# Feed-forward weight tiles laid out in DRAM along the loop, and three loads moved on the issue queue of a recurrent transformer block

## The chip, the cores and the metric

The kernel runs on one core of one Trainium2 chip. The metric is the device time of one launch in microseconds (us), as a median over several runs. The engines are TensorE (PE in the profile; PEld is its weight load), VectorE (DVE), ScalarE (ACT), GpSimd (POOL) and SyncE (SP), which here only issues DMAs.

## The reference

The input is one sequence of 2048 rows of 640 numbers in bf16. A pre-norm block is computed: recurrent attention over 64 segments of 32 rows, then a gated feed-forward part, each with a residual.

```python
x = A_x
h = x + _A_ref(_layernorm(x), A_mem0, A_Wq, A_Wk, A_Wv, A_Wo, 32)
h2 = h + _B_ref(_layernorm(h), B_W_gate, B_W_up, B_W_down)

def _A_ref(x, mem0, Wq, Wk, Wv, Wo, seg_len):      # 32 heads of 128
    mem = mem0                                      # 8 rows
    for s in range(n_seg):                          # 64 segments, one after the other
        h = concatenate([mem, xs], axis=1)          # 8 + 32 rows
        q, k, v = h @ Wq, h @ Wk, h @ Wv            # per head
        p = softmax(where(mask, q k^T * scale, -1e9))
        o = (p v) @ Wo
        mem = o[:, :M, :]                           # the next segment's memory
        outs.append(o[:, M:, :])

def _B_ref(x, W_gate, W_up, W_down):                # 640 -> 1728 -> 640
    gate = x @ W_gate
    return ((gate * (gate > 0)) * (x @ W_up)) @ W_down
```

Segment s needs the 8 memory rows that segment s-1 has put out, so the 64 segments are a chain.

## The kernel before, in words

A setup part loads the attention weights (W for Q, K and V, and Wo) into SBUF, where they stay, and computes segment 0. Then comes a loop over the steps s = 1 to 63, one segment each. After it the feed-forward part runs over four blocks of 512 rows.

**A step.** Each step projects K, Q and V for the segment (`project`, line 417; 390 is the same with another weight load), multiplies Q with K (`scores`, line 513), takes exponentials, and multiplies the probabilities of the memory rows with V (`pv_mem`, line 567). Then Wo is applied to the memory rows (`wo_split`, line 632, and `wo_pass`, line 615), and the result becomes the memory rows of the next step. The segment's own rows are not urgent: their probabilities meet V in `pv_x` (line 710), early in the next step, which reads V out of a rearranged copy called VM. Three DMAs (`merge_v(s, 0)`) write VM out of Vp as soon as V of the step is there, and where s % 4 = 2 three more (`merge_v(s, 1)`) write the other part out of Ve.

**Groups of four.** The last 8 rows of segments are projected four segments at a time, in steps where TensorE would otherwise wait, and wait in Ke, Qe and Ve. There are two sets of these: set 0 has tiles of its own, set 1 lies in one tile called ends. `place(s)` tells which set a step uses. Where s % 4 = 1, the step also turns a block of 128 normalized rows over (`flip_rows(at, xl)`, a DMA transpose), then loads the next rows into xl, and multiplies the last four segments' ends with Wo (`woe_pass`); the sum goes from the tile Pbd to DRAM by two DMAs (`woe_store`, called here the Pbd stores). `store_attn` stores the attention rows of every step by four DMAs.

**Feed-forward work inside the loop.** Nine pairs of tiles of the gate and up weights (128 of 1728 columns each) are multiplied with the first 512 normalized rows already in the loop, in steps 50, 51, 52, 54, 55, 56, 58, 59 and 60 (EARLY_STEPS; `early_product`, line 916). For that the 512 rows (xn2_d in DRAM, 5 chunks) are loaded over a set of Ke, Qe and Ve that is not in use: `early_rows` in the steps before, 49, 53 and 57. `early_weights(s, 0)` loads a gate tile into xt, `early_weights(s, 1)` an up tile into at (into xl in the last three). Each reads 640 rows of 256 bytes out of a weight matrix. The product with all chunks of the gate tile stands after the first `pv_mem`, the first chunk of the up tile after the second one, and the rest after `wo_pass`. As the row loads destroy what Ke, Qe and Ve held, saved copies in DRAM are brought back: K and Q by `load_next(q, n)` out of next_d, V out of farvw_d or nextv_d, in steps 53 and 57.

**What sets the order.** Every operation is given to one list in the order of the program. Each engine carries out its own part of that list in order; waits on semaphores are worked out from what the operations read and write (`_Graph.solve`). All DMAs inside the loop are issued by SyncE (line 355, transposes 378), so a DMA whose wait isn't over holds up every later one. One of them has its place tied by hand: the load behind `first_exp` (`after`) waits for the first exponential of its step.

**DRAM-to-DRAM copies.** Some copies run from DRAM to DRAM along the loop and stand at the end of their steps: four for the last 64 columns of gate and up (wt_d, steps 3, 6, 7, 10) and three that build farvw_d (steps 11, 14, 15).

## Time and profile before

| | before |
|---|---|
| median of 3 runs | 978.67 us (977.9 to 978.81) |
| profiled execution | 980.6 us, span 978.9 us |
| TensorE busy, share of the span | 954.4 us, 98% |
| VectorE / ScalarE / GpSimd busy | 74% / 53% / 19% |
| granted TensorE clock | 1.00 |
| DMA: moved, share of 16 engines | 89.00 MB, mean 91 GB/s; SyncE's queue 30.1% |

The profile gives one execution. A busy time counts an engine's instructions; a wait is an idle stretch, put down to whatever ended it. "issue" is idle time that ended without anything the profile shows. The chain that ended last is the work followed back from the last instruction, at each step to what released it. In a list in order of time the first column is the start in us from the span's start and the second the length; SPq is SyncE's issuing of a DMA, whose landing comes later. In a table of stretches the columns are the stretch, its length, each engine's busy time with its number of instructions, the granted clock, the share of the 16 DMA engines, and GB/s.

### The profile page before, as it was taken

Reading aid. Unit: us, or ns where it says so; the run is one execution under the profiler, and the core shown is the slowest. Engines: PE = TensorE matmul, PEld = TensorE weight load, DVE = VectorE, ACT = ScalarE, POOL = GpSimd, SP = SyncE. Lnnn points to the kernel's source line nnn. Section 1 sums busy time; section 2 is a strip of 40 time slices with the busy share of each in tenths; the row PEclk is TensorE's granted clock in tenths of the full one; section 3 lists DMA queues with packets and bytes.
Section 4 is the critical chain, followed back from the end, with each engine's and each line's share of the span. In section 5 each row is a group of like instructions: output and inputs, shape, how many; then the busy total and the mean of one; then the engine's idle time right before and its main releaser. Section 6 shows DMA issues by size and latency. Waiting matters only on the chain.

```text
span 978.9 us, 56709 instructions
## 1 busy us (share of the span) xinstructions
PE 954.4 (98%) x26155; PEld 532.9 (54%) x24915; DVE 726.8 (74%) x2041; ACT 522.7 (53%) x1326; POOL 186.7 (19%) x424
## 2 busy tenths in 40 slices
PE   4899999999999999999999999999999999999998
PEld 1245555556565556665556565656565655344443
DVE  3568888888888888888888888887887884445232
ACT  1466666666666666666666666655555553122120
POOL 7021112121313131313131313020201110000000
PEclk9999999999999999999999999999999999999999
DMA  9951212222232223222232323142424247704000
GB/s 362 416 219 51 46 46 44 55 43 64 50 74 52 65 55 62 57 68 57 63 60 57 61 57 61 37 101 62 133 60 132 61 131 234 263 18 98 21 14 28
DMA packets 94708, 89.00 MB, mean 91 GB/s; under 512 B 57386, under 2 KB 78066, under 8 KB 92402
## 3 DMA queue, kind: packets, MB, share of 16 engines
q1 hardware_dynamic: 92736, 84.41, 30.1%
q8 instruction: 201, 3.29, 1.5%
q10 hardware_dynamic: 1730, 0.96, 0.4%
q14 instruction: 41, 0.34, 0.1%
HBM read 47.80 MB, written 12.27 MB: 61 GB/s over the span
## 4 chain that ended last, share of the span: by engine, by line
PE 93%; SPq 4%; DMA 3%; issue 0%; DVE 0%; POOL 0%; ACT 0%; POOLq 0%
PE ps L417 46%; PE ps L1041 9%; PE ps L615 7%; PE ps L390 7%; PE ps L632 7%; PE ps L681 4%; SPq L355 4%; PE ps L1364 3%; PE ps L916 3%; PE ps L513 3%; PE ps L710 2%; DMA Wo<-in_A_Wo_dram 2%; PE ps L567 1%; PE ps L1054 0%; DMA VM<-Vp 0%
## 5 line engine op out<-in xcount | busy, mean ns | idle before, releaser
L417 PE MATMUL ps<-W,act_r 128*32 128x512 bf16 (+1 forms) x8335 | 466.1, 360 | 0.7 <-issue 0.4
L417 PEld LDWEIGHTS ps<-W,act_r 128*32 128x32 bf16 x8335 | 217.3, 96 | 168.4 <-issue 22.8
L441 ACT ACTIVATE tok<-ps 128x512 bf16<-128x512 f32 x184 | 106.4, 594 | 62.6 <-PE ps L417 48.7
L441 ACT ACTIVATE tox<-ps 128x512 bf16<-128x512 f32 x138 | 81.8, 598 | 60.9 <-PE ps L417 50.2
L436 DVE STREAM_TRANSPOSE Ko<-tox 128x512 bf16<-128x512 bf16 x128 | 89.0, 697 | 29.7 <-ACT tox L441 29.0
L417 PE MATMUL ps<-W,act_e 128*32 128x512 bf16 x1008 | 97.0, 382 | 4.3 <-DVE TBf L494 1.9
L595 DVE STREAM_TRANSPOSE oT<-tox 128x512 bf16<-128x512 bf16 x128 | 95.2, 744 | 0.0
L436 DVE STREAM_TRANSPOSE Qo<-tok 128x512 bf16<-128x512 bf16 x124 | 85.5, 690 | 2.0 <-ACT tok L441 1.2
L615 PE MATMUL ps<-Wo,oT 128*32 128x160 bf16 x4032 | 81.9, 233 | 2.1 <-DMA Wo<-in_A_Wo_dram 1.1
L632 PE MATMUL ps<-Wo,oT 128*32 128x320 bf16 x2016 | 79.9, 299 | 0.4 <-DVE oT L589 0.4
L615 PEld LDWEIGHTS ps<-Wo,oT 128*32 128x32 bf16 x4032 | 70.3, 97 | 13.0 <-DMA Wo<-in_A_Wo_dram 3.0
L441 ACT ACTIVATE Vp<-ps 128x512 bf16<-128x512 f32 x127 | 75.1, 592 | 0.5 <-ACT Vp L441 0.5
L390 PE MATMUL ps<-W,act_e 128*32 128x512 bf16 x712 | 70.1, 383 | 0.0
L1069 ACT ACTIVATE g<-ps 128x512 bf16<-128x512 f32 x43 | 25.0, 594 | 78.3 <-PE ps L1041 76.8
L648 ACT ACTIVATE SA<-TA 64x40 f32<-64x40 f32 x126 | 29.6, 235 | 65.2 <-DVE TA L645 64.5
L529 ACT ACTIVATE Pm<-ps 128x64 bf16<-128x64 f32 x126 | 28.3, 224 | 67.6 <-PE ps L513 66.4
L589 DVE STREAM_TRANSPOSE oT<-om 128x128 bf16<-128x128 bf16 x126 | 39.3, 312 | 31.1 <-ACT om L581 31.1
L513 PE MATMUL ps<-Qo,Ko 128*32 128x40 bf16 x2048 | 61.4, 181 | 0.0
L632 PEld LDWEIGHTS ps<-Wo,oT 128*32 128x32 bf16 x2016 | 50.9, 96 | 18.2 <-DVE rm L579 0.8
L513 PEld LDWEIGHTS ps<-Qo,Ko 128*32 128x32 bf16 x2048 | 46.7, 94 | 25.5 <-DVE Qo L436 18.0
L521 POOL COPY Qo<-ends 128x256 bf16<-128x256 bf16 x32 | 14.1, 439 | 239.9 <-DVE oT L589 232.8
L521 POOL COPY Qo<-Qe 128x256 bf16<-128x256 bf16 x32 | 14.2, 444 | 231.6 <-DVE oT L589 231.6
(156 smaller groups left out, 1550.1 us busy)
## 6 DMA issues: line engine op xcount, KB each, us to landing
VM<-Vp SPq DMA_DIRECT2D x126, 65.0 KB
VM<-Vp SPq DMA_DIRECT2D x63, 130.0 KB
W<-in_A_Wk_dram SPq DMA_DIRECT2D x5, 1024.0 KB
W<-in_A_Wq_dram SPq DMA_DIRECT2D x5, 1024.0 KB
W<-in_A_Wv_dram SPq DMA_DIRECT2D x5, 1024.0 KB
Wo<-in_A_Wo_dram SPq DMA_DIRECT2D x8, 640.0 KB
attn_d<-wtok SPq DMA_DIRECT2D x248, 7.5 KB
xt<-in_A_x_dram SPq DMA_DIRECT2D x16, 160.0 KB
```

Of the source, the lines that this page charges most:

```text
L355: add(eng, lambda e: e.dma_start(dst, src), r=r, w=w, dma=True)
L390: return pe.add_instruction(mybir.InstMatmult(name=nc.get_next_instruction_name(), engine=mybir.EngineType.PE, ins=[pe.lower_ap(rhs), pe.l ...
L417: ins = pe.matmul(*b, start=(c == ends[0]), stop=(c == ends[1]), skip_group_check=True)
L436: add("dve", lambda v: v.transpose(dst[:, 16 * i:16 * i + 16, 0:32], tok[t][:, :].rearrange("p (h f) -> p h f", f=32)), r=tok_keys(t), w=keys)
L441: add("act", lambda a: a.activation(dst, src, ACTF.Copy), r=r, w=w)
L513: i = pe.matmul(bank((P0, P1)[hf])[q:q + 32, o:o + 40], (Ko if a == 0 else Ke[p])[:, h, :], Qo[:, h, :], start=True, stop=True, skip_group ...
L589: add("dve", lambda v: v.transpose(ap(oT[par], 160 * hf, [[40, 4], [320, 4], [1, 8]]), ap(om, 128 * hf, [[1, 4], [4, 32]])), r=[("om", hf) ...
L595: add("dve", lambda v, kh=kh: v.transpose(ap(oT[p], 160 * kh + M, [[320, 4], [40, 4], [1, 32]]), ap(tox, 128 * kh, [[256, 4], [1, 4], [4, ...
L615: i = pe.matmul(bank(bk)[32 * gg:32 * gg + 32, 0:160], src[:, hb, 0:32], w[:, gg], start=(hb == CH[16 * halves[0]]), stop=(hb == CH[-1]), ...
L632: i = pe.matmul(bank(bk)[32 * q:32 * q + 32, 0:320], src[:, hb, 0:32], w, start=(n == 0), stop=(n == 7), skip_group_check=True)
L681: ins = pe.matmul(bank(bk)[32 * q:32 * q + 32, 0:320], src[:, hb, 0:32], w[:, 2 * (q % 2):2 * (q % 2) + 2], start=(i == 0), stop=(i == 15) ...
L1041: ins = pe.matmul(bank(bk), w[:, c, lo:lo + 128], xn2T[par][:, c, :], start=(c == 0), stop=(c == DC - 1))
```

## The change

1. A DRAM tensor we_d takes the nine pairs of weight tiles in the order in which a load wants them (one row of 1280 bytes a partition). Eighteen DRAM-to-DRAM copies fill it, one in each of the steps 18 to 40 where s % 4 is not 1. `early_weights` reads from it, 128 rows of 1280 bytes instead of 640 of 256.
2. The seven existing DRAM-to-DRAM copies and the eighteen new ones are issued by `lay_out(s)`, right behind `merge_v(s, 0)`.
3. In steps 53 and 57 both `load_next` (Q, then K) stand at the head of the step; before, K was loaded in its middle.
4. In steps 49, 53 and 57 the last two of three `early_rows` (chunks 0 and 1, and chunk 4) move from the middle of the step to behind the Pbd stores, ahead of the four attention stores.
5. In step 1 the store of ends moves behind the four other stores there.

```diff
+    we_d = nc.dram_tensor("we_d", [128, NE, 2, D], BF16)
...
     def early_weights(s, q):
-        (t, k), src = early_tile(s, q), (B_W_gate, B_W_up)[q]
+        t, k = early_tile(s, q)
         j = EARLY_STEPS.index(s)
-        dma(chunks_of(t[:, :]), src[:, 128 * j:128 * j + 128].rearrange("(c p) f -> p c f", p=128), w=[k])
+        dma(t[:, :], we_d[:, j, q, :], r=[("we_d", j, q)], w=[k])
...
+    WIDE = (11, 14, 15)
+    WEIGHTS = tuple(k for k in range(18, 41) if k % 4 != 1)
+
+    def lay_out(s):
+        if s in TAILS:
...
+        elif s in WIDE:
...
+        elif s in WEIGHTS:
+            j, q = divmod(WEIGHTS.index(s), 2)
+            dma(chunks_of(we_d[:, j, q, :]), (B_W_gate, B_W_up)[q][:, 128 * j:128 * j + 128].rearrange("(c p) f -> p c f", p=128),
+                w=[("we_d", j, q)])
...
                 early_weights(s, 1)
-            elif s == NSEG - 11:
-                load_next(1, 1)
-            elif s == NSEG - 7:
-                load_next(0, 1)
+            elif s in (NSEG - 11, NSEG - 7):
+                for n in (1, 0):
+                    load_next(int(s == NSEG - 11), n)
...
             elif s == 1:
-                dma(ends_d[:, :], ends[:, :], r=END_KEYS, w=[("ends",)])
                 far_save(0)
                 far_save(1)
                 for i in range(2):
                     dma(farv_d[:, 512 * i:512 * i + 512], tok[2 + i], r=tok_keys(2 + i), w=[("farv", i)])
+                dma(ends_d[:, :], ends[:, :], r=END_KEYS, w=[("ends",)])
...
         merge_v(s, 0)
+        lay_out(s)
         pv_mem(s, 0)
...
         if s in (NSEG - 15, NSEG - 11, NSEG - 7):
-            early_rows(1 - place(s + 1)[0], 0, 2)
-            early_rows(1 - place(s + 1)[0], 4, DC)
             if s == NSEG - 7:
                 early_weights(s + 1, 1)
-                load_next(0, 0)
                 dma(ap(Ve[0], 0, [[1, 8 * VW]]), nextv_d[:, :], r=[("nextv",)], w=[("Ve1", 0), ("Ve", 0, 0), ("Ve", 0, 1)])
             elif s == NSEG - 11:
-                load_next(1, 0)
...
-        if s in TAILS:
...
-        if s == 11:
...
-        if s in (14, 15):
...
         if woe:
             woe_sum(BQ[0])
             woe_store(s // 4 - 1)
+            if s in (NSEG - 15, NSEG - 11, NSEG - 7):
+                early_rows(1 - place(s + 1)[0], 0, 2)
+                early_rows(1 - place(s + 1)[0], 4, DC)
             store_attn(wtok, ("wtok",), M, 32 * (s - 1), RID)
```

More of the change, by code (lines that the diff above doesn't have):

```diff
@@ L1009, in build_kernel @@
     TAILS = (3, 6, 7, 10)
+    WIDE = (11, 14, 15)
+    WEIGHTS = tuple(k for k in range(18, 41) if k % 4 != 1)
+    def lay_out(s):
+        if s in TAILS:
+            q, e = divmod(TAILS.index(s), 2)
+            o = FR * (q ^ e)
+            dma(wt_d[:, e, :, o:o + FR], (B_W_gate, B_W_up)[q][:, FM:F].rearrange("(c p) f -> p c f", p=128), w=[("wt_d", q, e)])
+        elif s in WIDE:
+            i = WIDE.index(s) - 1
+            if i < 0:
+                dma(farvw_d[:, :], nextv_d[:, :], r=[("nextv",)], w=[("farvw", n) for n in range(2)])
+            else:
+                dma(farvw_d[:, 4 * VW * i:4 * VW * (i + 1)].rearrange("p (k d) -> p k d", d=VW)[:, :, 0:Dh],
+                    farv_d[:, 512 * i:512 * i + 512].rearrange("p (k d) -> p k d", d=Dh), r=[("farv", i)], w=[("farvw", i)])
+        elif s in WEIGHTS:
+            j, q = divmod(WEIGHTS.index(s), 2)
+            dma(chunks_of(we_d[:, j, q, :]), (B_W_gate, B_W_up)[q][:, 128 * j:128 * j + 128].rearrange("(c p) f -> p c f", p=128),
+                w=[("we_d", j, q)])
     def woe_sum(bk):
@@ L1320, in build_kernel @@
                 store_attn(wtok, ("wtok",), M, 32 * (s - 1), RID)
-        if s in TAILS:
-            q, e = divmod(TAILS.index(s), 2)
-            o = FR * (q ^ e)
-            dma(wt_d[:, e, :, o:o + FR], (B_W_gate, B_W_up)[q][:, FM:F].rearrange("(c p) f -> p c f", p=128), w=[("wt_d", q, e)])
-        if s == 11:
-            dma(farvw_d[:, :], nextv_d[:, :], r=[("nextv",)], w=[("farvw", i) for i in range(2)])
-        if s in (14, 15):
-            i = s - 14
-            dma(farvw_d[:, 4 * VW * i:4 * VW * (i + 1)].rearrange("p (k d) -> p k d", d=VW)[:, :, 0:Dh],
-                farv_d[:, 512 * i:512 * i + 512].rearrange("p (k d) -> p k d", d=Dh), r=[("farv", i)], w=[("farvw", i)])
         filler(2)
```

## The prediction

> **What bounds the kernel now.** I read the page's busy line, its instruction queue and its chain of waits first, then TensorE's waits by stretch, then the length of single steps, and last SyncE's issues in order of time in the steps that are too long. A step runs from the first product of one step's own-segment values (line 710) to the next step's.

> ```profile
> PE 954.4 (98%) x26155; PEld 532.9 (54%) x24915; DVE 726.8 (74%) x2041; ACT 522.7 (53%) x1326; POOL 186.7 (19%) x424
> q8 instruction: 201, 3.29, 1.5%
> PE 93%; SPq 4%; DMA 3%; issue 0%; DVE 0%; POOL 0%; ACT 0%; POOLq 0%
> ```

> TensorE is busy 954.4 of 978.9 us, and it is 93% of the chain that ended last. The other 7% (SyncE and DMA) are the weight loads ahead of the loop, which the change leaves alone. So an edit of DMAs inside the loop can only give back time in which TensorE stood still there. In order of time TensorE has five idle stretches worth naming between 600 and 800 us, and the view of its waits has none from 300 to 600 us (brackets: idle time before, and what ended it):

> ```profile
> 655.65 0.88 PEld L615 LDWEIGHTS ps<-Wo,oT 128*32 128x32 bf16 x52 [0.23 <-issue]
> 660.24 0.31 PE L710 MATMUL ps<-VM,Px 64*32 64x129 bf16 x16 [0.24 <-issue]
> 696.62 0.58 PE L710 MATMUL ps<-VM,Px 64*32 64x129 bf16 x32 [0.55 <-DMA VM<-Vp]
> 705.28 1.08 PE L615 MATMUL ps<-Wo,oT 128*32 128x160 bf16 x52 [0.32 <-issue]
> 750.19 0.61 PE L417 MATMUL ps<-W,act_r 128*32 128x512 bf16 x6 [0.36 <-issue]
> ```

> One is a wait for a DMA, four for nothing that the profile shows ("issue"); they lie in steps 50, 51, 54 (two) and 58. The lengths of steps (second column) tell the whole loss. Quiet steps 22, 23 and 8 come first (8 holds one of the small DRAM-to-DRAM copies that exist already), then 50, 51, 53, 54, 55 and 58:

> ```profile
> 312.61:324.56 11.95, 11.95 (x385) 6.83 (x361) 10.42 (x31) 8.01 (x21) 3.62 (x4) 1.00 0.35 69
> 324.56:336.49 11.93, 11.93 (x393) 7.32 (x374) 10.22 (x30) 7.51 (x19) 1.11 (x3) 1.00 0.27 72
> 144.90:156.86 11.96, 11.96 (x391) 7.00 (x370) 9.24 (x28) 7.51 (x19) 1.11 (x3) 1.00 0.15 36
> ...
> 647.50:659.69 12.19, 12.17 (x375) 7.09 (x363) 9.84 (x30) 7.52 (x20) 3.62 (x4) 1.00 0.32 82
> 659.69:672.06 12.37, 12.12 (x383) 7.14 (x380) 9.73 (x29) 7.02 (x18) 1.11 (x3) 1.00 0.26 65
> 683.98:696.62 12.64, 12.09 (x404) 7.51 (x397) 10.63 (x33) 7.36 (x19) 2.91 (x10) 1.00 0.52 142
> 696.62:709.31 12.69, 12.37 (x371) 7.31 (x363) 9.47 (x29) 6.91 (x20) 3.62 (x4) 1.00 0.44 122
> 709.31:721.24 11.93, 11.93 (x383) 7.19 (x380) 9.70 (x29) 7.03 (x18) 1.11 (x3) 1.00 0.28 68
> 745.21:758.10 12.89, 12.53 (x376) 7.23 (x363) 9.63 (x29) 7.02 (x18) 1.13 (x3) 1.00 0.43 117
> ```

> Against 11.95 (11.93 for 51; I take 11.99 for 53, whose kind is a little longer), steps 50, 51, 53, 54 and 58 lose 0.24 + 0.44 + 0.65 + 0.74 + 0.94 = 3.0 us. That is all the change can win: 0.31%. The granted clock (third from last) is 1.00 everywhere.

> What the "issue" waits are can be read from counts: matmuls and weight loads from the end of each of the four to the end of the next.

> ```profile
> 655.65:660.24 4.59, 4.34 (x127) 2.59 (x126) 3.07 (x10) 2.68 (x7) 0.74 (x3) 1.00 0.30 66
> 660.24:705.28 45.04, 44.17 (x1406) 26.74 (x1393) 36.70 (x108) 25.73 (x69) 8.25 (x19) 1.00 0.36 97
> 705.28:750.19 44.91, 44.55 (x1406) 26.31 (x1393) 36.09 (x104) 26.20 (x67) 4.14 (x12) 1.00 0.37 97
> ```

> That is 253, 2799 and 2799 instructions. The page's instruction queue moved 201 packets for 26155 + 24915 = 51070 of them, 254 a packet: the stalls lie 1, 11 and 11 packets apart. I read them as TensorE running out of instructions because a packet of them came late behind the DMAs of these steps (DMA share 0.43 to 0.52 in 53, 54 and 58, against 0.15 to 0.35 in quiet ones; but only 0.32 and 0.26 in 50 and 51).

> **The change part by part: the wait for VM.** In steps 53 and 54 SyncE and the critical chain show this:

> ```profile
> 684.54 1.45 SPq L355 DMA_DIRECT2D ends<-next_d  x1
> 686.39 1.25 SPq L378 DMA_TRANSPOSE at<-xl  x1
> 689.66 0.55 SPq L355 DMA_DIRECT2D xl<-in_A_x_dram  x1
> 691.45 1.85 SPq L355 DMA_DIRECT2D VM<-Vp  x3
> 696.38 1.33 SPq L355 DMA_DIRECT2D attn_d<-Pbd  x2
> 697.75 2.66 SPq L355 DMA_DIRECT2D attn_d<-wtok  x4
> 700.46 0.41 SPq L355 DMA_DIRECT2D at<-in_B_W_up_dram  x1
> ...
> 692.69 3.83 DMA VM<-Vp
> ```

> VM leaves SyncE at 691.45 because the load of xl may only follow the transpose that reads xl, and it lands 3.83 us after its last issue, at 696.52, 0.55 us late. The change puts the second load of next_d (Ke) ahead of that transpose: one more issue of about 0.45 us, and 256 KB more ahead of it in the queue. So VM leaves up to 0.45 us later. Against that the gate tile between xl and VM shrinks from 640 pieces of 256 B to 128 rows of 1280 B. Queued behind this waiting are the gate tile, the rows, VM and all of the step's stores. Bounds on the wait of 0.55 (0.65 with the slower products after it): minus 0.65 to plus 0.6; I take plus 0.1, near the issue's side.

> **Rows behind the Pbd stores.** Two row loads leave the middle of steps 49, 53 and 57 and go between the Pbd stores and the attention stores, early in the next step. They are needed by the first gate product there; the up tile behind them is needed 1.2 us later. In step 50:

> ```profile
> 646.51 1.34 SPq L355 DMA_DIRECT2D attn_d<-Pbd  x2
> 647.89 2.72 SPq L355 DMA_DIRECT2D attn_d<-wtok  x4
> 650.65 0.39 SPq L355 DMA_DIRECT2D at<-in_B_W_up_dram  x1
> 651.09 1.83 SPq L355 DMA_DIRECT2D VM<-Ve  x3
> 653.57 1.78 SPq L355 DMA_DIRECT2D VM<-Vp  x3
> ...
> 644.12 1.74 SPq L355 DMA_DIRECT2D ends<-xn_d  x2
> ...
> 652.75 1.26 PE L916 MATMUL ps<-ends,xt 128*32 128x512 bf16 x20
> 653.93 0.40 PE L916 MATMUL ps<-ends,at 128*32 128x512 bf16 x4
> ```

> Two row issues take 1.74 us here, about 1.2 without the one long issue among them. SyncE has no gap between the Pbd stores and the up tile, so the up tile leaves at 651.85 to 652.4 instead of 650.65, and TensorE wants it at 653.93. It did not wait before, so the load takes at most 3.28 us. A load of 3.28 us makes TensorE wait 1.2 to 1.75 us; one of 1.5 us or less costs nothing. I take 0.6, a landing after some 2.4 us. The rows themselves leave about 647.9 and have nearly 5 us until 652.75, longer than VM's 3.83 us in the fullest step: nothing. VM<-Ve moves by the same 1.2 to 1.75 us, from 651.09 to at most 652.8, and VM<-Vp then leaves at about 654.7 instead of 653.57; with 3.83 us after its last issue it lands by 660.3, at the edge of need, but step 50 is also lengthened by the wait. Nothing. In step 53 to 54 two issues (Ke<-next_d and the rows) no longer stand ahead of the Pbd stores, so these leave when their data is ready (11.0 us into the step, as in step 49, 694.98 here instead of 696.38). The two rows eat that up again: the up tile leaves about when it did, nothing. In step 58 there is no up tile at the head.

> **Stalls for instructions.** With 512 pieces fewer per tile and less traffic bunched in the middle of 53 and 57, fewer packets of instructions should be late. Step 50: its 0.24 goes, the up tile now being late instead, which leaves 0.6 - 0.24 = plus 0.36. Step 51: 0.44 goes, minus 0.4. Step 54: of the 0.5 that is left beside the VM wait I take half, minus 0.3 (bounds minus 0.5 to plus 0.5, the rows now falling there). Step 58: its stall followed Ke<-next_d, Ve<-nextv_d and the Pbd stores; the rows take the place of Ke, so of 0.94 I take away 0.6 (bounds minus 0.94 to plus 0.3).

> **The new copies.** Eighteen DRAM-to-DRAM copies of 160 KB, in steps 18 to 40 (never in a step with s % 4 = 1), stand on SyncE's queue right behind VM. The nearest rows are the small copy of step 8 (80 KB in the same 640 pieces, step length 11.96, which is the length of its kind) and the gate loads of steps 50, 51, 54, 55, 58 and 59, at the very place where the copies will stand; step 55, with such a load at its head too, has 11.93. The worst that I can lay to such a load is the stall in step 51 (0.44 us), after the gate load of step 50. So a copy costs 0 to 0.44 us, together 0 to 7.9; I take 0.2 in all, since of six such loads one was followed by a stall, in traffic that the quiet steps mostly don't have. The move past other work on the queue is felt most where s % 4 = 2:

> ```profile
> 320.53 1.28 SPq L378 DMA_TRANSPOSE at<-xt  x1
> 324.03 0.60 SPq L355 DMA_DIRECT2D xn_d<-at  x1
> 324.68 3.05 SPq L355 DMA_DIRECT2D attn_d<-wtok  x4
> 330.69 1.81 SPq L355 DMA_DIRECT2D VM<-Vp  x3
> ```

> The copy goes ahead of at<-xt: 0.6 us of issue and its own pieces. SyncE then waits longer for that transpose, and the store of xn_d and four attention stores wait behind it. They end at 327.73 now and VM leaves at 330.69, so there are 3 us in hand against perhaps 2. Nothing, unless that is gone: then VM of six steps is late.

> **Small moves.** The copies for the tails and for farvw move from a step's end to behind VM in steps 3 to 15, and the store of ends moves behind four others in step 1. No step there is lengthened by these now; 0, within 0.2 either way.

> **The sum.** 0.1 + 0.36 - 0.4 - 0.3 - 0.6 + 0.2 = minus 0.64 us. The profiled execution has a span of 978.9 and took 980.6 us; the median of the three runs is 978.67, 0.2% less. I take the difference off the median: 978.0 us. Changes below 0.2% (1.96 us) are about what a measurement of this kernel can't tell from none.

> [...]

> **The rivals.** *The stalls stay.* If the four stalls have nothing to do with how many pieces or loads stand ahead, only the new waits count: 0.1 + 0.6 + 0.2 = plus 0.9, 979.6 us. For it: step 55 has the same tile loads and no stall, so pieces alone don't make one. Against it: all long steps lie where rows and next_d are loaded, or just behind. Chance 0.17.

> *Faster: all of it goes.* VM lands in time and the up tile within 1.5 us: minus 3.0 and plus 0.2, 975.9 us. For it: VM is late by only 0.55, 3.0 us is a sum of short stalls. Against it: one more load ahead of the transpose in step 53, two ahead of the up tile in step 50. Chance 0.25.

> *Slower: the copies starve TensorE of instructions.* Every copy falls where TensorE crosses a packet boundary (one each 4 us, by 254 instructions of the 746 to 801 of a step). If each costs 0.25, the smallest stall seen, that is 4.5 us and 982.3 us with the other terms at minus 0.84; at 0.44 each it is 7.9 and 985.7. It decides from 0.16 us a copy on (1.96 + 0.84 over 18). For it: the stall in 51 came after such a load. Against it: 55 and 8. Chance 0.16.

> **How the numbers follow.** The forecast, a gain of parts of the stalls eaten up by new waits, has 0.42. Faster by over 0.2%: the second rival and a little of the forecast's edge, 0.26. Slower by over 0.2%: the third and a little of the first, 0.17. Within: 0.57. The range goes from the second rival, 975.6, to the top of the first, 980.6; what it leaves out is the slower rival. The forecast's own range is 977.0 to 979.2.

> **What would show it.** Right: no wait for VM above 1 us; a new wait of TensorE at line 916 in step 50, before the first product with at; step 51 at 11.93; steps 18 to 40 at 11.93 to 12.0. Wrong: steps of kinds 0, 2 and 3 between 18 and 40 longer by 0.2 or more (the copies); or steps 50, 54 and 58 all at 11.95 (all gone); or 51, 54 and 58 unchanged (the stalls have another cause).

## The result, and the profile after

| | before | after |
|---|---|---|
| median of 6 runs each | 978.28 us (977.29 to 979.95) | 982.45 us (980.69 to 983.03) |
| ratio, 95% interval | | 1.004 (1.0027 to 1.0053) |
| profiled execution | 980.6 us, span 978.9 us | 983.03 us, span 981.3 us |

The changed kernel is slower by 0.3 to 0.5%; forecast were 978.0 us and no measurable change. Timed twice more, the same kernel gave ratios of 1.0005 (0.9986 to 1.0024) and 1.0023 (1.0012 to 1.0034). Two of the three intervals leave out 1: there is a loss, nearer 0.2% than 0.4%, and a single timing of this kernel tells little below that.

The page of the changed kernel, with its busy line, DMA total, instruction queue and chain of waits:

```profile
PE 954.4 (97%) x26144; PEld 535.0 (55%) x24915; DVE 726.8 (74%) x2041; ACT 522.4 (53%) x1326; POOL 186.0 (19%) x424
DMA packets 97300, 91.95 MB, mean 94 GB/s; under 512 B 57674, under 2 KB 80658, under 8 KB 94994
q8 instruction: 201, 3.29, 1.4%
PE 90%; SPq 4%; DMA 4%; DVE 1%; issue 0%; ACT 0%; POOL 0%; DVEq 0%; ACTq 0%; POOLq 0%
```

TensorE is busy for the same 954.4 us in a longer span. The DMAs move 2.95 MB more (91.95 against 89.00), which is the eighteen copies of 160 KB. TensorE's share of the chain falls from 93 to 90%: it stands still more. Where, the long stretches tell (length in the second column, then TensorE's busy time): steps 18 to 48, which hold all eighteen copies, and 49 to 63, first of the changed kernel,

```profile
265.11:635.58 370.47, 370.47 (x12036) 222.09 (x11574) 318.36 (x927) 235.58 (x612) 94.31 (x164) 1.00 0.28 67
635.58:818.39 182.81, 179.98 (x5664) 109.32 (x5599) 142.86 (x412) 103.66 (x267) 25.90 (x62) 0.99 0.35 98
```

then of the kernel before:

```profile
264.78:635.51 370.73, 370.73 (x12036) 222.47 (x11573) 318.45 (x927) 235.78 (x612) 94.52 (x164) 1.00 0.26 59
635.51:815.79 180.28, 178.78 (x5664) 107.76 (x5598) 142.57 (x412) 103.64 (x267) 26.04 (x62) 1.00 0.38 100
```

Steps 18 to 48 have no idle time and are 0.26 us shorter. Steps 49 to 63 are 2.53 us longer. The steps that were too long in the prediction (50, 51, 53, 54 and 58), now after the change:

```profile
647.59:660.76 13.17, 12.17 (x375) 7.13 (x363) 9.85 (x30) 7.51 (x20) 3.61 (x4) 1.00 0.37 106
660.76:672.68 11.92, 11.92 (x382) 7.03 (x378) 9.68 (x29) 7.02 (x18) 1.10 (x3) 1.00 0.24 68
...
684.61:698.52 13.91, 12.16 (x404) 8.04 (x396) 11.68 (x34) 7.95 (x21) 3.25 (x11) 1.00 0.43 124
698.52:712.49 13.97, 13.89 (x371) 7.79 (x362) 8.89 (x27) 6.42 (x17) 3.22 (x4) 0.88 0.39 115
...
748.36:760.51 12.15, 12.15 (x376) 7.07 (x364) 9.63 (x29) 7.02 (x18) 1.12 (x3) 1.00 0.39 112
```

Step 50 went from 12.19 to 13.17, 53 from 12.64 to 13.91, 54 from 12.69 to 13.97: plus 3.53. Steps 51 and 58 gained 0.45 and 0.74. TensorE's waits between 600 and 815 us name the two loads behind this:

```profile
PE ps L711 <- DMA VM<-Vp: 1.8, 1, 1.8
PE ps L917 <- DMA at<-we_d: 1.0, 1, 1.0
```

The four "issue" waits of before are gone, and two waits for DMAs stand in their place: VM 1.8 us late instead of 0.6, and the up tile, which was in time before, 1.0 us late. The loop from step 2 to step 63 is 744.71 us long here against 742.54, plus 2.2. Step 1 is counted with the head: it is 13.18 us long against 12.28, with a wait of 1.18 us for VM at its end. The change moves stores in that step, but the kernel before, profiled a second time, has 13.09 there too. In all, the two profiled executions are 2.4 us apart. The rest of the 4.2 us between the medians is mostly that the profiled execution of the kernel before was itself 2.3 us above its median.

### The profile page after: what moved, and what is told of

Same layout as the page of the kernel before. It is cut to its first block, busy times and chain, and to the rows that moved or that the text cites. A ratio compares the mean times of both kernels' runs of the same rounds, so it can differ in the third digit from the quotient of the medians.

```text
span 981.3 us, 56716 instructions
## 1 busy us (share of the span) xinstructions
PE 954.4 (97%) x26144; PEld 535.0 (55%) x24915; DVE 726.8 (74%) x2041; ACT 522.4 (53%) x1326; POOL 186.0 (19%) x424
## 2 busy tenths in 40 slices
DMA packets 97300, 91.95 MB, mean 94 GB/s; under 512 B 57674, under 2 KB 80658, under 8 KB 94994
## 3 DMA queue, kind: packets, MB, share of 16 engines
q8 instruction: 201, 3.29, 1.4%
## 4 chain that ended last, share of the span: by engine, by line
PE 90%; SPq 4%; DMA 4%; DVE 1%; issue 0%; ACT 0%; POOL 0%; DVEq 0%; ACTq 0%; POOLq 0%
PE ps L418 45%; PE ps L1061 9%; PE ps L616 7%; PE ps L391 7%; PE ps L633 7%; SPq L356 4%; PE ps L682 3%; PE ps L1373 3%; PE ps L514 2%; PE ps L711 2%; PE ps L917 2%; DMA Wo<-in_A_Wo_dram 2%; PE ps L568 1%; DMA Wt<-wt_d 1%; DMA VM<-Vp 1%; PE ps L1074 0%
```

## The experiments

**One part undone at a time.** Three kernels each take one part of the change back, and a fourth takes back K, the rows and the order in step 1, so that only the copies, the loads from we_d and their place are left.

*K back in the middle of its step:*

```diff
-            elif s in (NSEG - 11, NSEG - 7):
-                for n in (1, 0):
-                    load_next(int(s == NSEG - 11), n)
+            elif s == NSEG - 11:
+                load_next(1, 1)
+            elif s == NSEG - 7:
+                load_next(0, 1)
...
+                load_next(0, 0)
...
             elif s == NSEG - 11:
+                load_next(1, 0)
```

> The changed kernel with one part undone: the load of K stands in the middle of steps 53 and 57 again, only Q at their head. Theory A (the second load ahead of the transpose makes VM late in step 53): the wait of TensorE for VM at the start of step 54 falls from 1.75 us back to about 0.55 us, the clock stays at full speed behind it, and the time falls by 1.2 to 2.9 us against the changed kernel, to some 0.15 to 0.25% above the kernel before. Rival B (the rows behind the Pbd stores are what costs): the wait for VM stays above 1.2 us, and the time stays about 0.4% above before. Rival C (the copies along the loop cost): no change here either.

Measured: 979.40 us, ratio 1.0002 (0.9990 to 1.0013). That is less than the 0.15 to 0.25% expected, but the interval leaves a microsecond open either way; the waits are in the profile. Step 53 is 12.00 us long, VM in time. Its steps 50 and 54, and TensorE's waits from 600 to 815 us:

```profile
648.09:661.54 13.45, 12.17 (x377) 7.13 (x364) 9.85 (x30) 7.52 (x20) 3.62 (x4) 1.00 0.36 103
697.39:710.82 13.43, 12.17 (x376) 7.10 (x364) 9.98 (x31) 7.52 (x20) 3.62 (x4) 1.00 0.44 128
```
```profile
PE ps L917 <- DMA at<-we_d: 2.5, 2, 1.3
```

With K back the VM wait is gone, and the rows alone make TensorE wait 1.3 us for the up tile, in step 50 and in step 54 alike.

*Rows back in the middle of their step:*

```diff
         if s in (NSEG - 15, NSEG - 11, NSEG - 7):
+            early_rows(1 - place(s + 1)[0], 0, 2)
+            early_rows(1 - place(s + 1)[0], 4, DC)
...
-            if s in (NSEG - 15, NSEG - 11, NSEG - 7):
-                early_rows(1 - place(s + 1)[0], 0, 2)
-                early_rows(1 - place(s + 1)[0], 4, DC)
             store_attn(wtok, ("wtok",), M, 32 * (s - 1), RID)
```

> The changed kernel with the two row loads of steps 49, 53 and 57 back in the middle of their steps. Theory B: the wait of TensorE for the up tile in step 50 (1.0 us) goes, and the time falls by about 1 us against the changed kernel (some 0.1%); steps 53 and 54 stay long, since K is still at the head, and VM may come later still (rows ahead of nothing, but two more issues in the middle). Theory A alone would leave it 0.4% above before; if the rows were the main cause it would come within 0.1% of before.

Measured: 979.89 us, ratio 1.0009 (0.9998 to 1.0020). The mirror image: step 50 is 12.48 and the up tile in time; VM is as late as in the changed kernel. Step 53, and the waits:

```profile
683.01:696.84 13.83, 12.06 (x403) 7.52 (x396) 11.52 (x34) 7.96 (x21) 3.31 (x11) 1.00 0.45 123
```
```profile
PE ps L711 <- DMA VM<-Vp: 1.8, 1, 1.8
PE ps L616 <- issue: 0.3, 1, 0.3
```

*The store of ends first again in step 1:*

```diff
             elif s == 1:
+                dma(ends_d[:, :], ends[:, :], r=END_KEYS, w=[("ends",)])
                 far_save(0)
...
-                dma(ends_d[:, :], ends[:, :], r=END_KEYS, w=[("ends",)])
```

> The changed kernel with the store of ends ahead of the four other stores of step 1 again. If the place of that store makes VM late in step 1 (a wait of 1.18 us in the changed kernel, none before), step 1 falls from 13.18 to about 12.3 us and the time by about 0.9 us. If the wait comes from how the transposes and the stores happen to fall, step 1 stays long in some executions whatever the order, and the time does not move.

Measured: 980.78 us, ratio 1.0015 (1.0003 to 1.0027), as the changed kernel. Steps 50, 53 and 54 are 12.82, 13.87 and 13.62 long. Step 1, for which the run was made, is still 12.96 long with a wait of 0.92 us. In the kernels without added instructions it is 12.8 to 13.5 us, whatever the order of these stores, but for the 12.28 of the first profile of the kernel before. So their order is no part of the loss that the profiles show.

*The layout alone (K, rows and ends all as before):* the three diffs above together.

> The layout alone: copies along the loop and loads from the laid-out tiles, with K, the rows and the store of ends where they were before. If the moved loads are the whole loss (theories A and B), this is not slower than before: steps 18 to 40 at 11.93 to 12.0 us, steps 50 to 58 a little shorter than before, a ratio of 0.997 to 1.000. If the copies cost (rival C), it is 0.2 to 0.4% slower, with longer steps between 18 and 40 or a longer head or tail.

Measured: 979.15 us, ratio 0.9998 (0.9987 to 1.0008). Steps 18 to 48 and 49 to 63:

```profile
265.05:635.69 370.64, 370.64 (x12036) 221.94 (x11573) 318.45 (x927) 235.87 (x612) 94.55 (x164) 1.00 0.29 67
635.69:814.65 178.96, 178.22 (x5665) 108.23 (x5600) 142.37 (x412) 103.69 (x267) 26.04 (x62) 1.00 0.36 101
```

So neither the eighteen copies nor the tiles laid out as rows of 1280 B move the time by anything that this run can show. What the steps lose, they lose with the two moves.

**How much of the picture of before was one execution?** The kernel before, unchanged, with a new profile, and the changed kernel with two:

> The kernel before, profiled on the same chip: shows how much of the head (up to step 2) and the tail (after step 63) moves between executions of one program. Expected: a ratio of 1.000; steps 50, 51, 53, 54 and 58 long by 0.2 to 1 us each as in its first profile; head and tail each different by up to 1 us from that.

> The changed kernel once more, so that the others of this chip can be compared with it. Expected: 0.2 to 0.4% slower than before; steps 50, 53 and 54 some 13 to 14 us long by the waits for the up tile and for VM, steps 18 to 40 unchanged at 11.93 to 12.0 us.

> The changed kernel a third time: its ratio to before was 1.004 in the first measurement and 1.0005 in the second. The loop alone was 2.3 us longer in the profiles (0.23%). Expected 1.001 to 1.003; above or below it would mean that the head and the tail, which the change does not touch, move it.

Measured: the kernel before 978.93 us (0.9993, 0.9973 to 1.0014), the changed one 980.46 and 981.01. In the kernel before, steps 49 to 63 and TensorE's waits there are now:

```profile
635.05:814.18 179.13, 178.46 (x5664) 108.41 (x5599) 142.47 (x412) 103.70 (x267) 26.06 (x62) 1.00 0.37 101
```
```profile
PE ps L710 <- DMA VM<-Vp: 0.4, 1, 0.4
```

None of the four "issue" waits is there, against what was expected. Steps 50, 51 and 58 are 11.98, 11.93 and 12.18 long instead of 12.19, 12.37 and 12.89, with nothing changed; 53 and 54 stay long (12.54 and 12.89). More than a third of the 3.0 us on which the prediction rested belonged to that one execution. Over all profiles of the two kernels the loop is 742.5 and 741.3 us in the kernel before (mean 741.9), and 744.7, 743.8 and 742.6 in the changed one (mean 743.7): 1.8 us, or 0.2%, which is what the three timings say together. The second timing (0.05%) fell short of the 0.2 to 0.4% expected of it, the third met its range.

The third profile of the changed kernel shows that the two waits are separate events. Its steps 53 and 54, and the waits:

```profile
685.50:697.50 12.00, 12.00 (x403) 7.47 (x395) 10.03 (x31) 6.85 (x18) 2.91 (x10) 1.00 0.54 151
697.50:710.78 13.28, 12.17 (x375) 7.13 (x362) 9.97 (x31) 7.51 (x20) 3.61 (x4) 1.00 0.40 114
```
```profile
PE ps L917 <- DMA at<-we_d: 2.3, 2, 1.2
```

VM is in time here, and step 53 is at its quiet length. Step 54 is long all the same, by the up tile.

**Why VM is late.** SyncE in step 53 of the changed kernel, issues in order of time (start, duration):

```profile
685.18 1.66 SPq L356 DMA_DIRECT2D ends<-next_d  x2
686.89 1.26 SPq L379 DMA_TRANSPOSE at<-xl  x1
692.36 0.54 SPq L356 DMA_DIRECT2D xl<-in_A_x_dram  x1
692.94 0.59 SPq L356 DMA_DIRECT2D xt<-we_d  x1
693.57 1.35 SPq L356 DMA_DIRECT2D Qe<-xn_d  x1
694.97 1.84 SPq L356 DMA_DIRECT2D VM<-Vp  x3
```

The issue of K costs little: the transpose is issued 2.28 us into the step, before at 2.41. But its end comes late. SyncE's wait for it is the row that decides, first in the kernel before, then in the changed kernel's three profiles in order:

```profile
SPq L124 <- DMA at<-xl: 2.0, 1, 2.0
```
```profile
SPq L124 <- DMA at<-xl: 4.1, 1, 4.1
```
```profile
SPq L124 <- DMA at<-xl: 3.9, 1, 3.9
```
```profile
SPq L124 <- DMA at<-xl: 1.9, 1, 1.9
```

It is 3.4 with the rows back, 3.5 with the store of ends first, and 1.8 to 2.0 in all four profiles with K in the middle (two of the kernel before, K back alone, layout alone). Everything behind (xl, the gate tile, Qe, VM) waits with it: VM leaves 10.4 us into the step instead of 7.5. So with K ahead SyncE waits 1.4 to 2.3 us longer, in four of five profiles. In step 57, where K is ahead too, no profile shows a wait for VM.

The bytes of K are not what the transpose waits for. This is the busy share of the 16 DMA engines in the recorded profile of the changed kernel, in tenths, in 40 slices from 684 to 700 us:

```profile
DMA  0020810139999910000000006573069985388733
```

From 690.0 to 693.6 us the engines are less than a tenth busy, and the signals of the transpose come at 692.14 to 692.29. What stands in between, the records of single DMA packets show. The instruction queue moved 201 packets of 16 KB in this execution (3.29 MB, 1.4% of the 16 engines' time; the count further down makes them TensorE's), and one runs from 689.55 to 691.08. Seventeen small packets of SyncE's queue follow at its end, the last of them at 691.51, and then nothing is left to do. In the three other late profiles all parts of the transpose but one are done by the time that the instruction packet ends; one 4-byte packet starts within 0.02 us of that end, and the last signal comes about a microsecond later. By these times the transpose is late where an instruction packet holds up its last part. With K in the middle such a packet starts at the same place, some 5 us into the step, and none of four profiles shows the delay. That K ahead makes the meeting likelier rests on four of five profiles against none of four.

The test is to put both loads right behind the transpose:

```diff
-            elif s in (NSEG - 11, NSEG - 7):
-                for n in (1, 0):
-                    load_next(int(s == NSEG - 11), n)
...
                 flip_rows(chunks_of(at[:, :]), xl, ("xl",), ("at",))
+                if s in (NSEG - 11, NSEG - 7):
+                    for n in (1, 0):
+                        load_next(int(s == NSEG - 11), n)
```

> The changed kernel with one thing moved: in steps 53 and 57 Q and K are loaded right behind the transpose of xl, not ahead of it. Theory A says that the loads ahead make the transpose land at some 7.5 us into step 53 instead of 5.5 and VM leave 3 us late. Then the transpose now lands by 4 us, VM leaves at about 6.8 us and TensorE waits for it 0 to 0.5 us instead of 1.75; steps 53 and 54 lose some 1.8 to 3 us of their 27.9, step 50 keeps its wait for the up tile. If the load of the queue as a whole and not the order ahead of the transpose made VM late, the same bytes in the same step would keep the wait at 1 us or more.

Measured: 979.40 us, ratio 1.0000 (0.9983 to 1.0018). SyncE's wait, then steps 53 and 54:

```profile
SPq L124 <- DMA at<-xl: 0.3, 1, 0.3
```
```profile
683.95:696.34 12.39, 12.24 (x403) 8.09 (x395) 10.10 (x31) 6.86 (x18) 2.92 (x10) 1.00 0.54 156
696.34:708.33 11.99, 11.99 (x376) 7.25 (x364) 9.99 (x31) 7.53 (x20) 3.62 (x4) 1.00 0.41 117
```

The transpose is issued at 684.51, 0.56 us into the step, SyncE issues the two loads while it runs, and xl leaves at 688.26, 4.3 us into the step (7.8 in the changed kernel, 5.7 before). VM leaves at 6.1 and is in time. The transpose is over 4.1 us into the step here, and the instruction packet starts only at 5.8. So the place of the loads ahead of the transpose is what lets VM become late. This kernel takes both moves' loss away although the rows still stand behind the Pbd stores, and its step 50 is 12.15 long. The reason for that is on SyncE's queue in step 50. In the changed kernel:

```profile
646.60 1.32 SPq L356 DMA_DIRECT2D attn_d<-Pbd  x2
647.96 0.97 SPq L356 DMA_DIRECT2D ends<-xn_d  x2
648.97 2.81 SPq L356 DMA_DIRECT2D attn_d<-wtok  x4
651.82 0.35 SPq L356 DMA_DIRECT2D at<-we_d  x1
```

In the kernel with the loads behind the transpose:

```profile
648.31 0.96 SPq L356 DMA_DIRECT2D ends<-xn_d  x2
649.32 1.61 SPq L356 DMA_DIRECT2D attn_d<-wtok  x4
650.98 0.35 SPq L356 DMA_DIRECT2D at<-we_d  x1
```

Four attention stores take 1.61 us to issue, and 2.81 when one of the four is a long one. The rows cost 0.97 us; it takes both, the rows and a long issue, to make the up tile late. In the five other profiles with the rows and the up tile in these places and no products added (three of the changed kernel, K back, ends first) a long issue stands ahead of the up tile in step 50, and the tile is late in all five. So step 50 of this kernel is an escape by chance, not a mend.

Both the long issue and the late tile go with instruction packets again. Of the 37 issues of plain DMAs longer than 0.95 us between 100 and 815 us in the changed kernel's recorded profile, 36 end 0.2 to 0.5 us after the end of such a packet. In step 50, 15 of the 16 signals of the up tile come within 2.29 us of its issue, and the last one after 3.35 us; a packet ran from 0.89 to 2.04 us. In all nine cases in which TensorE waits for the up tile of step 50 or 54, a packet ran during the load, and the last signal came 1.1 to 1.5 us after the packet's end. In step 50 of the kernel with the loads behind no packet runs during the load, and all sixteen are there after 2.26 us.

**Both mended.** In addition the up tiles of steps 50 and 54 are issued ahead of the Pbd stores:

```diff
-            if s in (NSEG - 14, NSEG - 13, NSEG - 12, NSEG - 10, NSEG - 9, NSEG - 8, NSEG - 5, NSEG - 4):
+            if s in (NSEG - 13, NSEG - 12, NSEG - 9, NSEG - 8, NSEG - 5, NSEG - 4):
                 early_weights(s, 1)
...
+        if s in (NSEG - 15, NSEG - 11):
+            early_weights(s + 1, 1)
```

> As the run with the loads behind the transpose, and the up tiles of steps 50 and 54 are issued ahead of the Pbd stores of the steps before (49 and 53), as soon as the tile is free. Theories A and B together: no wait of TensorE for VM or for a tile from step 49 to 60, steps 50 to 58 at 11.93 to 12.2 us; against the changed kernel minus 4 to 5 us in the loop, against the kernel before minus 2 to 3 us, a ratio of 0.997 to 0.999. If the stalls that the profile calls issue come back or copies along the loop cost, it ends at 1.000 or above.

Measured: 979.07 us, ratio 0.9993 (0.9976 to 1.0009). Steps 50, 53 and 54 are 12.51, 12.50 and 11.99 long. No wait for the up tile is left, but the loop isn't 2 to 3 us shorter than before, as was expected: steps 50 and 53 are longer than 12.2 us mostly by busy time (12.39 and 12.24). The same with the rows back in the middle:

> The layout with everything that cost undone or moved again: Q and K behind the transpose, the rows in the middle of their steps as in the kernel before, the up tiles of steps 50 and 54 ahead of the Pbd stores. If the waits for VM and for the up tile are all that the change cost, and the layout itself is worth something, no step from 49 to 60 is longer than 12.5 us, the loop is 1 to 2 us shorter than before and the ratio is 0.998 to 0.999. If what is left of the long steps of before comes from where instruction packets end, and not from the tile loads, it is 1.000 as with the layout alone.

Measured: 979.57 us, ratio 1.0002 (0.9986 to 1.0019); steps 50, 53 and 54 are 11.98, 12.51 and 11.98 long, the loop 741.4 us. Both take the loss away and neither beats the kernel before: 741.4 to 741.8 us of loop is about what its second profile had too (741.3), and of the two outcomes that the last expectation names, the second came.

**Are the "issue" waits packet boundaries?** The prediction read them as late packets of instructions. If so, their place follows from the count of TensorE's instructions. 96 small products (with their weight loads 192 instructions) ahead of TensorE's first own one move every later boundary and compute nothing that is used; once on the changed kernel, once on the one before:

```diff
+    def early_blocks(pe):
+        for _ in range(96):
+            i = pe.matmul(bank(T1)[:, 0:32], ident[:], ident[:, 0:32], start=True, stop=True, skip_group_check=True)
+        return i
+    add("pe", early_blocks, r=[("ident",)], w=[B(T1)])
     row_stats(xt, ("xt",), HEAD, [("xt", "late")])
```

> The changed kernel with 96 small products (192 instructions) ahead of the first one, where TensorE waits for x anyway. They change nothing in the loop but the place where TensorE's instruction packets of 256 end: all of them 192 instructions, some 3 us, earlier in a step. If the transpose of step 53 lands late because a packet of instructions meets it on one of the DMA engines (at 4.9 to 5.3 us into the step in all profiles so far), it now lands before 6.3 us, VM leaves a microsecond or more earlier and the wait for VM in step 53 falls below 1 us. If the two loads ahead alone make it late, it lands at 7.3 to 7.7 us as before, and the wait stays at 1.4 to 1.8 us.

> The kernel before with the same 192 instructions ahead. If the waits that the profile calls issue are TensorE running out of instructions at the end of a packet, they now stand at other places: counted in matmuls and weight loads, 192 earlier (or 64 later) than in the profiles of before, so none at the sixteen products behind the scores of step 58, where it was. The step lengths of 50, 51, 54 and 58 change by some tenths either way, the total stays within 0.1% of before. If something else makes these waits (a semaphore that the profile misses), they stay where they were.

Measured: 989.85 us on the changed kernel (1.0122 of the kernel before, 1.0102 to 1.0142) and 991.14 on the one before (1.0128, 1.0110 to 1.0145). Without the products they took 981.01 and 979.09 on the same chip, so the shift costs 8.8 and 12.1 us. The products themselves stand in the head, which is hardly longer for it (72.2 and 74.1 us, against 73.7 and 73.3 in the recorded profiles). The loss is in the loop. Steps 18 to 48, and the largest group of "issue" waits of the whole run (total, number, longest), on the changed kernel:

```profile
265.45:642.59 377.14, 374.01 (x12037) 231.91 (x11574) 318.57 (x927) 235.79 (x612) 94.23 (x164) 1.00 0.31 65
```
```profile
PE ps L616 <- issue: 7.5, 12, 1.2
```

On the kernel before:

```profile
266.81:641.96 375.15, 373.73 (x12036) 230.32 (x11573) 318.68 (x927) 235.76 (x612) 94.30 (x164) 1.00 0.26 58
```
```profile
PE ps L615 <- issue: 4.0, 9, 1.2
```

The same instructions in the same order, 4.4 to 6.7 us longer in steps that had no idle time, with and without the copies. Partly it is idle time put down to "issue", partly the busy times of products and weight loads grow. The second expectation had put the total within 0.1%, and missed it more than tenfold.

That these are waits for packets can be counted. With the semaphore instructions on its queue TensorE has 51449 records in the profile of the kernel before, 256.0 for each of the 201 packets. Counted so, of the 35 "issue" waits of 0.15 us or more in its products from step 2 to 63 of all profiles, 34 stand at one place of a packet: 193 instructions past a multiple of 256 without the added products, 191 with them. (The one that doesn't is a wait of 0.6 us in the kernel with both mended.) Each of these 34 ends 1.2 to 1.6 us after the end of an instruction packet on the DMA engines, where packets come 4.0 us apart. So the waits are for the next packet, as the prediction read them. Why some packets come late, and why so many more with the shift, these runs don't show. DMA traffic alone isn't the reason, since the shift brings the waits into quiet steps (a DMA share of 0.31 and 0.26 in steps 18 to 48, against 0.28 and 0.26 without it).

The first expectation came only in part. On the changed kernel with the products SyncE's wait for the transpose is 2.0 us and VM leaves 8.0 us into the step instead of 10.4, but TensorE still waits 1.06 us for VM. On the kernel before with them it is 1.19 us, with K in the middle and a wait for the transpose of 2.1. In both the issues of the transpose and of the gate tile are long (2.23 and 1.08 us, 1.80 and 1.56). So a late transpose is one way to a late VM and not the only one.

## Why the prediction was wrong

**The wait for VM (plus 0.1, bounds minus 0.65 to plus 0.6): the step that failed.** It priced K as one more issue on SyncE, and took the gate tile's shorter landing against it. The issue was cheap, as priced. What it left out is that the end of the transpose could move: it put nothing for that beside the issue. With K ahead its last part met a packet of TensorE's instructions in four of five profiles, and SyncE's wait for it grew from 2.0 us to between 3.4 and 4.1. VM's wait went from 0.55 to between 1.4 and 1.8 us in the first two profiles on the changed kernel, and in those with the rows or with the store of ends undone, plus 0.8 to 1.2, beyond the upper bound; in the third it was gone. The sign to look at was in the row quoted then: the transpose was issued at 686.39 and xl only at 689.66, so SyncE already stood there for 2 us.

**Rows behind the Pbd stores (plus 0.36 net, wait of 0.6): right path, mis-sized.** The new wait at the first product with at in step 50 came, as "What would show it" said: 0.5 to 1.3 us in the profiles of the changed kernel and of K back alone. The up tile left at 651.82, where 651.85 to 652.4 was forecast. Its landing was put at 2.4 us. The wait on record ends with this product:

```profile
655.22 0.40 PE L917 MATMUL ps<-ends,at 128*32 128x512 bf16 x4 [1.00 <-DMA at<-we_d]
```

It started 3.40 us after that issue, a little over the upper bound of 3.28 worked out from before. The 2.4 us were right for fifteen of the sixteen parts (2.29 us); the term was too small by the sixteenth, which came at 3.35, 1.3 us after the end of an instruction packet. By these numbers the tile would have been just in time without it: 651.82 + 2.3 is 654.1, and TensorE wanted it at 654.22. The long rows bring the fifteen parts some 0.3 us earlier (2.1 to 2.35 us in steps 50 and 54 with them, 2.4 to 2.7 in the two profiles of the kernel before), which the last part hides. And *step 54, priced at nothing*, was wrong. "The up tile leaves about when it did" counted the two issues that no longer stand ahead of the Pbd stores against the two rows. But the Pbd stores left only 0.4 us earlier against the start of step 54 (with K back), since their data wasn't ready, and the rows took 1.7 us, a long issue among them: the up tile leaves 4.5 us into step 54, against 3.8 before, and TensorE waits for it as in step 50. In both later profiles of the changed kernel, with K back and with ends first that wait is 1.1 to 1.3 us; in the recorded one no packet met the tile, which was there 2.20 us after its issue, and step 54 was slow for another reason (below). That is a second wait of the same size which the sum hadn't.

**Stalls for instructions (minus 0.4, minus 0.3, minus 0.6).** Steps 51 and 58 did lose 0.45 and 0.74. But the unchanged kernel lost them too when profiled again, so the change didn't win them: the ceiling of 3.0 us was read from one execution. The rival *the stalls stay* was nearest in kind (new waits count, the stalls aren't the change's to give), and too small for the same two prices: 0.9 us instead of about 1.8.

**The copies (plus 0.2; bounds 0 to 7.9) and the small moves (0): right.** With the layout alone the ratio is 0.9998, and steps 18 to 48 stayed at 370.4 to 370.7 in every profile with the copies and without added instructions. The rival *the copies starve TensorE* gave 982.3 to 985.7 us, and the recorded median lies in there, by another cause: nothing of it lies in steps 18 to 48; it lies in 50, 53, 54 and, where the change can't be told from a second execution of the kernel before, in step 1.

**The rival *all of it goes*** fell with the same rows: VM and up tile were late by 1.75 and 1.00 us.

**Why the sum missed.** In place of 0.1 + 0.36 - 0.3 for VM, step 50 and step 54, the first profile has 1.27 + 0.98 + 1.28, which is 3.37 us more. The gains in steps 51 and 58 came out nearly as put, 0.45 + 0.74, by luck: the unchanged kernel has them too. Over all profiles the loop lost 1.8 us; the rest of the recorded 4.2 us, which two repetitions didn't show, isn't explained. The stated range, 975.6 to 980.6, ends 0.3 and 1.0 us beyond the sums of the two rivals from which it is taken (975.9 and 979.6), without a reason given.

## What to carry to other kernels

On a queue that issues in the order of the program a load that is moved forward can cost more than its issue: here it moved the end of a transfer that SyncE then waits for (a transpose whose source buffer is to be refilled; the wait grew from 2.0 us to between 3.4 and 4.1 in four of five profiles), and everything issued behind that wait moved with it (in the recorded profile VM left 10.4 us into the step instead of 7.5). The last part of a transfer is the one that counted: in step 50 of the changed kernel TensorE's first product with the up tile began 1.1 us after the fifteenth signal and 0.05 us after the sixteenth. That part came up to 2 us behind the others where a packet of instructions met the transfer, so in this kernel a load needs that much time in hand. Where a queue has no gap, ask of every load behind the insertion point how much time it has in hand, in each step where the move takes place, and count the longest issue seen, not the usual one. Before a plan is built on waits of a few tenths of a microsecond, profile the same kernel a second time: what isn't there again can't be won.

## What the runs showed of the hardware

```profile
698.52 0.73 PE L711 MATMUL ps<-VM,Px 64*32 64x129 bf16 x32 [1.75 <-DMA VM<-Vp]
699.17 2.29 PE L418 MATMUL ps<-W,act_r 128*32 128x512 bf16 x20
```
```profile
699.24:701.47 2.23, 2.23 (x25) 0.74 (x24) 0.90 (x2) 0.00 (x0) 1.38 (x1) 0.50 0.64 189
701.89:703.20 1.31, 1.31 (x21) 0.45 (x12) 1.06 (x3) 0.84 (x3) 0.00 (x0) 0.70 0.12 29
703.20:704.00 0.80, 0.80 (x35) 0.43 (x29) 0.69 (x2) 0.60 (x1) 0.00 (x0) 1.00 0.26 43
```

Twenty products take 2.29 us; in the next profile of the same kernel, after a wait of 1.36 us and at full clock, the same twenty take 1.26. The sixteen behind them take 1.54 instead of 1.04. So this one late load cost 1.75 us of waiting and some 1.5 us of slow products: that is why step 54 is as long as 13.97 here, with a busy time of 13.89, although the up tile is in time. The clock fell after an idle stretch of 1.75 us in this profile, and not after 1.8 us at the same place in two others (rows back and ends first), whose granted clock is 1.00. What decides between them the runs don't show.

**The last of sixteen.** In three of the four profiles in which the transpose is late, 15 of the 16 signals of its end have come by 5.6 to 5.8 us into the step, and only the last one at 7.3 to 7.6; in the recorded one all sixteen come at 7.5 to 7.7. The load of xl leaves behind the last one, in the recorded profile at 692.36 after a last signal at 692.29. The records don't name the engine of a packet. That the late part and the instruction packet share one is read from their times: in all four late profiles the last packets of SyncE's queue start within 0.02 us of the instruction packet's end. In the third profile of the changed kernel such a packet ran at the same time (from 4.9 us into the step) and the transpose was not late, so the meeting depends on more than the time.

**The place of 192 instructions is worth about 1%.** Put ahead of everything they cost 9 to 12 us, some five times what the whole change moved. A change of TensorE's instruction count in this kernel can so cost time for a reason that is in none of its parts.
